# Cutting the first two token tiles at 128 columns, the last tile at 288, and changing which semaphore the last multiply waits for itself: a fused attention and MLP block on one Trainium2 core

## The chip, the cores and the metric

The kernel runs on one core of one Trainium2 chip. The metric is the device time of one execution in microseconds (us); the kernel before takes 141.5 us (median of 3 runs, 141.45 to 141.58). The span of a profile, from the first to the last instruction, is about 1.6 us shorter than that time (139.6 us in a run of 141.24). No other core works; the granted clock is 0.999 or 1.0. The engines are TensorE (PE), VectorE (DVE), ScalarE (ACT), GpSimd (POOL) and SyncE (SP). TensorE's weight loads are called PEld.

## The reference, cut to what matters

```python
xn  = layernorm(x)                                  # x: 1 x 2048 x 448, bf16
q, k, v = split(xn @ wqkv)                          # 16 heads of 28
pq, pk = phi(q), phi(k)                             # phi(t) = (t + 1 if t > 0 else exp(t)) + 1e-6
s   = (pq @ (pk.T @ v)) / (pq @ sum(pk)) @ wo       # linear attention, per head
g   = silu(relu(xn @ w1 + b1)**2 @ w2 + b2)         # hidden width 1792
out = x + s * g
```

## The kernel before

The kernel is a small program of operations with reads and writes. A list scheduler with modelled durations sets the order of the work on VectorE, ScalarE and GpSimd, and the PSUM bank of each result; TensorE's order is the order in the text. Three parts matter here.

**The head.** 16 tiles of 128 tokens. The first four tiles are normed on VectorE (the last 64 columns of tiles 0 and 1 on GpSimd), transposed on TensorE in chunks of 128 columns (0 to 3, the last only 64 wide) and copied from PSUM to SBUF as `xT`. In the first two tiles the norm of the first 384 columns is cut in two, so that TensorE can begin early. `k0`, `k1` are the key projections of tiles 0 and 1 (512 columns a matmul); `h_mains` are the first hidden units over both tiles (256 columns a matmul).

```python
def ln_norm(si, part=None):
    c = (slice(0, D if si > 3 else 384), slice(0, 256), slice(256, 384))[0 if part is None else part + 1]
    ...
reads = xn_of(t)[c // 2 :][:1] or xn_of(t) if c < 3 else [("xd", t)]      # which norm part a transpose waits for
...
warm(8, wide=True)                  # matmuls of ones, 512 columns each: the warm-up
turn("xT00", 0, (0,), "dve")        # transpose of tile 0 chunk 0, copied by VectorE
turn("xT01", 0, (1,), "act")
turn("xT02", 0, (2,), "act")
mains(k0, (0,), [("xT", 0, 0)] + wk0)
turn("xT10", 1, (0, 1), "act")
mains(k0, (1,), [("xT", 0, 1)])
turn("xT12", 1, (2,), "act")
mains(k0, (2,), [("xT", 0, 2)])
mains(k1, (0, 1), [("xT", 1, 0)] + wk0)
h_mains(0, (0, 1))
mains(k1, (2,), [("xT", 1, 2)])
...                                 # transpose of b1
h_mains(0, (2,))
turn("xT03", 0, (3,), "act", 2)
h_mains(1)
turn("xT2", 2, K3, "act")
h_mains(2)
turn("xT3", 3, K3, "dve")
h_mains(3)
turn("xT23", 2, (3,), "act", 2)
rests(k0, k1)                       # the first matmuls of 64 rows: in the trace two start 3 ns apart (8.598, 8.601 us)
```

**The waits.** The last tile's two multiplies wait in the trace for one semaphore themselves; the others are on a separate wait instruction ahead of each. The list `need` is ordered by modelled end, latest first, and the first of the list is the one that ends up on the instruction itself: the trace has ScalarE's semaphore on the last multiply, which starts at 137.336 us, and TensorE's on a separate wait at 137.270.

```python
for d in sorted(deps, key=lambda d: -d.end):
    ...
    need.append((d.sem, d.seq))
```

**The tail.** The last tile is done in two column parts, so that the second part's chain is short: bias matmul, silu on ScalarE, multiply by the attention part on VectorE, residual on VectorE, store.

```python
ca, cb = slice(0, 256), slice(256, D)
full(ss(14), KS, ["msz"])
full(gg(15, ca))
full(ss(15, ca, eng="dve", end=False), KS, ["msz"])
store(15, ca)
full(gg(15, cb, True), range(NF + 1))                     # ends with the bias matmul
full(ss(15, cb, eng="dve", end=False), KS, ["msz"])       # four matmuls of the attention part
store(15, cb, "act")
```

## Time and profile before

| what | value | from |
|---|---|---|
| time, median | 141.5 us | the runs |
| span of the profiled run | 139.6 us | page |
| TensorE busy | 98% of the span | page, part 1 |
| chain that ended last | 95% TensorE | page, part 4 |
| first transpose, first key matmul, first 64-row matmul | 4.19, 4.79, 8.60 us | timeline |
| last bias matmul, last store issued, all landed | 136.65, 138.02, 139.61 us | timeline |

The chain of the kernel before, by engine:

```profile
PE 95%; DVE 2%; DMA 2%; issue 0%; DVEq 0%
```

So time is to be had only where TensorE is not at work or works slowly. The records of single matmuls show no gap over 0.1 us between 8.6 and 137 us. What remains is the head and the tail. First the timeline of the head of the kernel before, VectorE's first norms and then TensorE, with lines left out: start in us, duration in us, engine, line, operation, out<-in, shape, count, and in brackets idle time before it.

```profile
3.82 0.59 DVE L488 TENSOR_SCALAR xn<-x_tok,mv,rstd 128x256 bf16<-128x256 bf16 x2
...
4.19 0.57 PE L531 MATMUL pb<-ident,xn 128*128 128x128 bf16 x3 [0.29 <-DVE xn L488]
4.79 0.54 PE L645 MATMUL pb<-w_qkv,xT 128*128 128x512 bf16 x1
5.17 0.28 PE L531 MATMUL pb<-ident,xn 128*128 128x128 bf16 x2
5.28 0.38 PE L645 MATMUL pb<-w_qkv,xT 128*128 128x512 bf16 x1
5.50 0.22 PE L531 MATMUL pb<-ident,xn 128*128 128x128 bf16 x1
5.55 0.97 PE L645 MATMUL pb<-w_qkv,xT 128*128 128x512 bf16 x3
6.36 0.38 PE L692 MATMUL pb<-xT,w 128*128 128x256 bf16 x2
...
8.60 0.39 PE L645 MATMUL pb<-w_qkv,xT 64*128 64x512 bf16 x2
```

The records of matmuls overlap: the one of 512 columns at 5.280 us lasts 0.379 us, and the next starts at 5.496, 0.216 us after it. So the distances between starts say more than durations. The warm-up matmuls, of 512 columns too, start 0.427 us apart (from 0.707 to 3.267 us). "Half clock" or "half rate" in this document means the distance of 0.427 us, "full clock" that of 0.216, and "the clock's rise" the moment when the one gives way to the other. The profile's own granted clock reads 1.00 in every stretch of the head (`--windows`), so that a clock lies behind the two distances is the author's reading and was not shown.

The first key matmul at 4.79 takes 0.37, to 5.17: the clock rose in the middle of it, at about 5.11 us by this arithmetic (an estimate: half rate, 0.427, up to there, full rate, 0.216, after). The three of 5.55 hide another wait: the records have the first at 5.552 and the second at 5.919, 0.151 us later than 0.216 would put it. That is the wait for ScalarE's copy xT10.

Then the tail of the kernel before, the timeline of ScalarE, VectorE and TensorE, with lines left out:

```profile
136.65 0.25 PE L958 MATMUL pb<-b2b,c 128*128 128x192 bf16 x1
...
136.94 0.33 ACT L935 ACTIVATE gbuf<-pb 128x192 bf16<-128x192 f32 x1 [0.80 <-PE pb L958]
...
137.34 0.36 DVE L995 TENSOR_TENSOR xn<-pb,gbuf 128x192 bf16<-128x192 f32 x1 [0.42 <-ACT gbuf L935]
137.73 0.26 DVE L1004 TENSOR_TENSOR xn<-xn,x_tok 128x192 bf16<-128x192 bf16 x1
138.02 0.37 ACTq L403 DMA_DIRECT2D out_dram<-xn  x1
```

The bias matmul ends, the silu follows, the multiply starts 0.070 us after the silu's end (records: 137.336 after 137.266), then residual and store. Just ahead of the multiply the records have a separate wait for TensorE's semaphore, at 137.270.

### The profile page before, as it was taken

How to read it: one execution, taken by the hardware profiler on the slowest of the kernel's cores; microseconds unless marked ns; L12 is line 12 of the kernel's file. 1: busy time of each engine (PE TensorE's matmuls, PEld its weight loads, DVE VectorE, ACT ScalarE, POOL GpSimd, SP SyncE). 2: the span in 40 equal slices, each digit the busy share in tenths (PEclk: the TensorE clock that was granted, in tenths of full speed). 3: DMA queues.
4: the chain of work that ended last, by engine and by line, in shares of the span. 5: the costliest groups of instructions: out<-in, count | busy, mean ns of one | idle time of the engine just before them, and what ended most of it. 6: DMA issues, size and time to landing. Idle time of an engine off the chain costs nothing.

```text
span 139.6 us, 3096 instructions
## 1 busy us (share of the span) xinstructions
PE 136.6 (98%) x1255; PEld 68.4 (49%) x1255; DVE 92.3 (66%) x225; ACT 78.3 (56%) x153; POOL 26.8 (19%) x35
## 2 busy tenths in 40 slices
PE   9999999999999999999999999999999999999993
PEld 2484444444444444444455455645555555555482
DVE  3989797898888996889995900217946072452743
ACT  4689789788988888979788912513033030300220
POOL 2810000000000000000893000000001429092670
DMA  6997546999722300000000149980000102112132
GB/s 207 238 335 212 94 152 171 359 285 149 130 52 58 64 9 5 0 19 5 0 0 0 34 115 161 159 137 7 0 0 5 66 0 97 40 62 69 36 100 66
DMA packets 20353, 12.90 MB, mean 92 GB/s; under 512 B 9524, under 2 KB 19956, under 8 KB 20340
## 3 DMA queue, kind: packets, MB, share of 16 engines
q1 hardware_dynamic: 18332, 11.52, 33.4%
q10 hardware_dynamic: 2008, 1.20, 4.6%
q8 instruction: 10, 0.16, 0.5%
q14 instruction: 3, 0.02, 0.1%
HBM read 8.78 MB, written 2.10 MB: 78 GB/s over the span
## 4 chain that ended last, share of the span: by engine, by line
PE 95%; DVE 2%; DMA 2%; issue 0%; DVEq 0%
PE pb L959 31%; PE pb L692 30%; PE pb L645 9%; PE pb L1025 8%; PE pb L726 7%; PE pb L676 6%; DMA x_tok<-in_A_x_dram 2%; PE pb L732 1%; PE pb L531 1%; DVE st L465 1%; PE pb L819 1%; PE pb L780 1%; PE pb L857 0%; DVE xn L995 0%; DVE mv L466 0%; PE pb L850 0%
## 5 line engine op out<-in xcount | busy, mean ns | idle before, releaser
L692 PE MATMUL pb<-xT,w 64*128 64x512 bf16 (+2 forms) x408 | 51.7, 365 | 0.0
L959 PE MATMUL pb<-w,r 64*128 64x448 bf16 (+3 forms) x406 | 44.9, 343 | 0.0
L701 ACT ACTIVATE r<-pb,b1f 128x512 bf16<-128x512 f32 x56 | 35.1, 689 | 3.7 <-PE pb L692 3.7
L692 PEld LDWEIGHTS pb<-xT,w 64*128 64x128 bf16 (+1 forms) x408 | 22.9, 94 | 22.2 <-ACT r L701 0.3
L959 PEld LDWEIGHTS pb<-w,r 64*128 64x128 bf16 (+1 forms) x406 | 22.8, 95 | 19.9 <-issue 0.7
L935 ACT ACTIVATE gbuf<-gbuf 128x448 bf16<-128x448 bf16 (+1 forms) x16 | 8.7, 566 | 36.0 <-DVE gbuf L970 35.5
L970 DVE TENSOR_TENSOR gbuf<-pb,b2b 128x448 bf16<-128x448 f32 (+1 forms) x16 | 9.2, 608 | 28.8 <-PE pb L959 28.8
L1004 POOL TENSOR_TENSOR xn<-xn,x_tok 128x448 bf16<-128x448 bf16 x15 | 15.0, 1032 | 46.3 <-DVE xn L995 46.3
L645 PE MATMUL pb<-w_qkv,xT 64*128 64x512 bf16 (+1 forms) x106 | 18.2, 378 | 0.0
L676 PE MATMUL pb<-xT,w_qkv 64*128 64x512 bf16 x84 | 15.5, 376 | 0.0
L709 DVE TENSOR_TENSOR r<-r 128x512 bf16<-128x512 bf16 x42 | 14.3, 416 | 0.0
L392 POOL MEMSET kvm<- 128x2048 bf16 x1 | 1.8, 1805 | 59.2 <-DVE zb L670 59.2
L1025 PE MATMUL pb<-msb,pqT 64*128 64x448 bf16 (+3 forms) x93 | 10.9, 343 | 0.0
L633 DVE SCALAR_TENSOR_TENSOR qk<-pb,qk 128x512 bf16<-128x512 f32 x16 | 10.6, 684 | 0.2
L465 DVE BATCH_NORM_STATS2 st<-x_tok 128x6 f32<-128x448 bf16 x16 | 9.3, 611 | 2.1 <-DMA x_tok<-in_A_x_dram 2.1
L623 ACT ACTIVATE qk<-pb 128x512 bf16<-128x512 f32 x16 | 8.9, 595 | 3.2 <-PE pb L645 2.7
L995 DVE TENSOR_TENSOR xn<-pb,gbuf 128x448 bf16<-128x448 f32 (+2 forms) x17 | 9.2, 590 | 2.0 <-ACT gbuf L935 1.5
L645 PEld LDWEIGHTS pb<-w_qkv,xT 64*128 64x128 bf16 (+1 forms) x106 | 6.7, 94 | 6.3 <-ACT xT L545 0.3
L726 PE MATMUL pb<-qk,xn 128*128 128x448 bf16 x48 | 9.3, 353 | 0.0
L676 PEld LDWEIGHTS pb<-xT,w_qkv 64*128 64x128 bf16 x84 | 6.0, 94 | 5.0
L710 ACT ACTIVATE r<-r 128x512 bf16<-128x512 bf16 x14 | 8.4, 636 | 0.0
L623 ACT ACTIVATE pqT<-pb 128x512 bf16<-128x512 f32 x12 | 6.8, 597 | 2.7 <-PE pb L692 1.6
(72 smaller groups left out, 101.9 us busy)
## 6 DMA issues: line engine op xcount, KB each, us to landing
out_dram<-xn SPq DMA_DIRECT2D x15, 112.0 KB, 1.7
w<-in_B_w_dram SPq DMA_DIRECT2D x1, 1568.0 KB, 9.9
x_tok<-in_A_x_dram SPq DMA_DIRECT2D x3, 448.0 KB, 3.7
xT<-rows ACTq DMA_DIRECT2D x6, 112.0 KB
w<-in_B_w_dram SPq DMA_DIRECT2D x1, 576.0 KB, 5.6
xT<-rows SPq DMA_DIRECT2D x5, 112.0 KB
w_o<-in_A_wo_dram SPq DMA_DIRECT2D x1, 392.0 KB, 11.0
w_qkv<-in_A_wqkv_dram SPq DMA_DIRECT2D x1, 384.0 KB, 3.4
```

The lines of the kernel that those rows point to most:

```text
L465: add("dve", lambda e, _: e.bn_stats(st6[:, si, :], x_tok[:, si, :]), [("x", si)], [("st", si)], 0.58),
L623: add("act", lambda e, _: e.activation(out=slot, in_=src(), func=AF.Exp), [buf, "actw"], [tile], 0.6)
L633: lambda e, _: e.scalar_tensor_tensor(out=slot, in0=src(), scalar=1.0 + 1e-6, in1=slot, op0=ALU.add, op1=ALU.max),
L645: return e.matmul(ps(b)[:, 0:512], xT[half[h], c, si * P : (si + 1) * P], w_qkv[half[h], c, 384 : 2 * D], start=start, stop=stop,)
L676: return e.matmul(ps(b)[:, 0:512], w_qkv[half[h], c, m * P : (m + 1) * P], xT[half[h], c, g * 512 : (g + 1) * 512], start=start, stop=stop,)
L692: return e.matmul(ps(b)[:, c0 : c0 + n], w_1[half[h], c, fi * P : (fi + 1) * P], xT[half[h], c, t : t + n], start=start, stop=stop,)
L701: lambda e, _: e.activation(out=slot, in_=ps(b)[:, 0:512], func=AF.Relu, bias=b1f[:, fi : fi + 1]),
L709: return e.tensor_tensor(out=slot, in0=slot, in1=slot, op=ALU.mult)
L726: last = e.matmul(ps(b)[:, 0:D], xn[:, si, c * P : (c + 1) * P], pk_of(si), start=(si == 0), stop=(si == NT - 1),)
L959: return e.matmul(ps(b)[:, 0:n], r2[half[h], fi, si * P : (si + 1) * P], w_2[half[h], fi, c], start=start, stop=stop)
L1004: eng, lambda e, _: e.tensor_tensor(out=ob, in0=ob, in1=x_tok[:, si, c], op=ALU.add),
L1025: return e.matmul(ps(b)[:, 0:n], q, m, start=start, stop=stop)
```

## The change

Its intent: TensorE should start earlier and in smaller steps in the head (the first norm has 128 columns instead of 256, and one transpose instead of two is due before tile 1's first copy). At the end the last part should be smaller (160 columns instead of 192), and the multiply should have TensorE's semaphore on itself, with ScalarE's on the separate wait.

```diff
-            for d in sorted(deps, key=lambda d: -d.end):
+            for d in sorted(deps, key=lambda d: (d.eng != op.lastly, -d.end)):
...
-            c = (slice(0, D if si > 3 else 384), slice(0, 256), slice(256, 384))[...]
+            c = (slice(0, D if si > 3 else 384), slice(0, P), slice(P, 384))[...]
...
-                reads = xn_of(t)[c // 2 :][:1] or xn_of(t) if c < 3 else [("xd", t)]
+                reads = xn_of(t)[min(c, 1) :][:1] or xn_of(t) if c < 3 else [("xd", t)]
...                                              # finish(): the multiply
+            if c.stop == D and c.start:
+                op.lastly = "pe"
...
-        turn("xT10", 1, (0, 1), "act")
+        turn("xT10", 1, (0,), "act")
         mains(k0, (1,), [("xT", 0, 1)])
-        turn("xT12", 1, (2,), "act")
+        turn("xT12", 1, (1, 2), "act")
         mains(k0, (2,), [("xT", 0, 2)])
-        mains(k1, (0, 1), [("xT", 1, 0)] + wk0)
-        h_mains(0, (0, 1))
-        mains(k1, (2,), [("xT", 1, 2)])
+        mains(k1, (0,), [("xT", 1, 0)] + wk0)
+        h_mains(0, (0,))
+        mains(k1, (1, 2), [("xT", 1, 1)])
...
-        h_mains(0, (2,))
+        h_mains(0, (1, 2))
...
-        ca, cb = slice(0, 256), slice(256, D)
+        ca, cb = slice(0, 288), slice(288, D)
```

More of the change, by code (lines that the diff above doesn't have):

```diff
@@ L45, in __init__ @@
         self.first = False
+        self.lastly = None
 class Acc:
@@ L484, in ln_norm @@
         def ln_norm(si, part=None):
-            c = (slice(0, D if si > 3 else 384), slice(0, 256), slice(256, 384))[0 if part is None else part + 1]
+            c = (slice(0, D if si > 3 else 384), slice(0, P), slice(P, 384))[0 if part is None else part + 1]
             return add(
@@ L492, in ln_norm @@
                 [("x", si), ("mv", si), ("rstd", si)], [("xn", si) if part is None else ("xn", si, part)],
-                0.4 if part is None else (0.22, 0.18)[part],
+                0.4 if part is None else (0.14, 0.24)[part],
             )
@@ L992, in finish @@
             n = c.stop - c.start
-            add(
+            op = add(
                 "dve",
```

## The prediction

> **What bounds the kernel.** The chain of waits is 95% TensorE. In the trace's matmul records I find no gap over 0.1 us between 8.6 and 137 us. So only the head (3.8 to 8.6 us) and the tail (after 136.6 us) can give time. The timeline of the head shows TensorE waiting 0.14 us (4.27 to 4.46), 0.27 us (4.52 to 4.79, for VectorE's copy xT00) and 0.15 us (5.77 to 5.92, for ScalarE's copy xT10); the first key matmul also takes 0.37 us instead of 0.216, because the clock is at half rate until about 5.1 us[...] (warm-up matmuls of 512 columns start 427 ns apart, later ones 216 ns). [...]
>
> **Head.** The norm of 256 columns takes 314 ns, of 384 columns 349: 0.27 ns a column, so 128 instead of 256 saves about 35 ns (estimate). The first transpose (4.19), the copy xT00 (4.51) and the first key matmul (4.79) come 35 ns earlier, of which the half-rate clock leaves about half. The transposes of chunks 1 and 2 both wait for the second norm part (done at 4.41 as now), so xT01's copy starts 0.17 us later, still before its use at 5.2. Tile 1: one transpose (56 ns) leaves the space before the second key matmul, and the copy xT10 falls from 384 to 272 ns, done at about 5.68; the 0.15 us wait at 5.77 goes. In exchange xT12's copy is 384 ns instead of 272, done at about 6.12: TensorE, with one chunk of the first hidden matmuls instead of two to fill with, waits a new 0.10 us before tile 1's second key matmul. Net: the transpose xT03 (6.96) moves to about 6.88. The weight loads have landed in time, xn3 (7.76, 50 ns before its use) moves up 35 ns, so 0.08 us should hold to 8.6 us and shift the dense part as a whole.
>
> **Tail.** TensorE's columns are the same in total; its last matmul ends about 13 ns earlier[...]. After the bias matmul come 4 matmuls of 160 columns (69 ns each) instead of 192 (82 ns); the silu falls from 331 to about 304 ns but starts 40 ns later, ending 14 ns later. Now TensorE's semaphore is waited for ahead of the last multiply (at 137.270), which starts 66 ns after, and ScalarE's (silu over at 137.266) on the instruction; a direct wait costs 33 ns after ScalarE. In the changed kernel TensorE arrives about 60 ns before ScalarE, and ScalarE's wait moves to the separate instruction: the multiply starts about 100 ns after silu's end, 45 ns later than now. Multiply (358 to 324) and residual (258 to 241) give 50 ns back. Tail: about -0.01 us. The swap alone looks like a loss of about 60 ns, hidden by the smaller part. The 288-column chain on VectorE ends near 137.23, just clear.
>
> **Sum.** -0.08 - 0.01: 141.4 us from 141.5, range 141.15 to 141.6. Faster by over 2%: 0.005; within 2%: 0.99; slower: 0.005.
>
> **Signs.** Timeline: first transpose near 4.15; no wait at 5.75 but one near 6.1; first 64-row matmul at 8.52 instead of 8.60; last multiply 320 ns, starting 0.10 us after silu's end.
>
> **What would make it wrong.** The scheduler orders VectorE's and ScalarE's work and the PSUM banks by modelled times; another order could give TensorE a wait in the dense part. The clock's rise could fall elsewhere. The 288-column chain might block the last multiply. The separate wait may cost less than 66 ns.

## The result, and the profile after

The changed kernel takes 141.29 us (median of 6 runs, 141.15 to 141.68), the kernel before 141.50 (6 runs, 141.38 to 141.58). The ratio is 0.999 with a 95% interval of 0.9976 to 1.0004. Ratios here are the mean time of one kernel's fast runs over that of the other's of the same rounds, so not quite the ratio of the medians. Executions over 1.5% slower than the fastest of the same kernel are left out of the means.

The profiled runs (141.24 us before, below all six of its timed runs, and 141.17 after) differ by 0.087 us from the first instruction to the landing of the last store. The order of the instructions on each engine differs only in the moved and resized pieces, so the scheduler did not reorder the dense part. The chain is still TensorE's:

```profile
PE 95%; DVE 2%; DMA 2%; ACT 0%; issue 0%; DVEq 0%
```

The timeline of the head of the changed kernel, the corresponding lines:

```profile
3.81 0.59 DVE L489 TENSOR_SCALAR xn<-x_tok,mv,rstd 128x128 bf16<-128x128 bf16 x2
...
4.15 0.70 PE L532 MATMUL pb<-ident,xn 128*128 128x128 bf16 x3 [0.25 <-DVE xn L489]
4.76 0.47 PE L646 MATMUL pb<-w_qkv,xT 128*128 128x512 bf16 x1
5.07 0.22 PE L532 MATMUL pb<-ident,xn 128*128 128x128 bf16 x1
5.12 0.38 PE L646 MATMUL pb<-w_qkv,xT 128*128 128x512 bf16 x1
5.34 0.28 PE L532 MATMUL pb<-ident,xn 128*128 128x128 bf16 x2
5.46 0.59 PE L646 MATMUL pb<-w_qkv,xT 128*128 128x512 bf16 x2
5.89 0.27 PE L693 MATMUL pb<-xT,w 128*128 128x256 bf16 x1
6.09 0.60 PE L646 MATMUL pb<-w_qkv,xT 128*128 128x512 bf16 x2
...
8.50 0.39 PE L646 MATMUL pb<-w_qkv,xT 64*128 64x512 bf16 x2
```

The first transpose comes 35 ns earlier. There is no wait inside the 5.46 group any more. A new one stands between 5.89 and 6.09: a matmul of 256 columns takes 0.109 us from start to start (6.593 to 6.702), so 0.097 us are idle (the copy xT12). The first key matmul takes 0.31 us to 5.07, not 0.37: the clock rose earlier in this run, at about 4.95 (estimated in the same way). The first 64-row matmul starts at 8.499 us instead of 8.598.

The tail of the changed kernel, the same lines of the timeline:

```profile
136.62 0.23 PE L959 MATMUL pb<-b2b,c 128*128 128x160 bf16 x1
...
136.89 0.30 ACT L936 ACTIVATE gbuf<-pb 128x160 bf16<-128x160 f32 x1 [0.59 <-PE pb L959]
...
137.30 0.33 DVE L996 TENSOR_TENSOR xn<-pb,gbuf 128x160 bf16<-128x160 f32 x1 [0.17 <-ACT gbuf L936]
137.66 0.24 DVE L1007 TENSOR_TENSOR xn<-xn,x_tok 128x160 bf16<-128x160 bf16 x1
137.94 0.37 ACTq L404 DMA_DIRECT2D out_dram<-xn  x1
```

The multiply now starts 0.103 us after the silu's end (137.301 after 137.198), not 0.070.

The 0.087 us, section by section, from the records of the two profiles:

| section | before, us | after, us | difference |
|---|---|---|---|
| to the first norm | 3.817 | 3.811 | -0.006 |
| first norm to first 64-row matmul | 4.781 | 4.688 | -0.093 |
| from there to the last bias matmul | 128.055 | 128.126 | +0.071 |
| bias matmul to issue of the last store | 1.365 | 1.310 | -0.055 |
| issue to landing seen | 1.591 | 1.587 | -0.004 |

In the third row, 0.053 us is only a shift: 18 matmuls of the first part (14 of the MLP, 4 of the attention) have 32 columns more and 14 of the second part have 32 fewer, and 128 columns take 0.053 us (a matmul of 512 columns takes 0.216 us from start to start, one of 256 takes 0.109, so 128 columns more are half of 0.107). e2 and e12, which have the split, show 128.109 in this row. The other 0.018 arises at about 16.7 us, where one of two matmuls that run side by side starts 0.017 us later than in e2. So the tail as a whole, third row's shift included, gained about 0.002 us, and the head gained 0.093 in this pair of profiles. The experiments ask whether the head's part belongs to the change, and why a smaller last part gained nothing.

### The profile page after: what moved, and what is told of

Its sections match the earlier page's. It is cut to its first block, busy times and chain, and to the rows that moved or that the text cites. A ratio compares the mean times of both kernels' runs of the same rounds, so it can differ in the third digit from the quotient of the medians.

```text
span 139.5 us, 3096 instructions
## 1 busy us (share of the span) xinstructions
PE 136.6 (98%) x1255; PEld 72.4 (52%) x1255; DVE 92.3 (66%) x225; ACT 78.3 (56%) x153; POOL 26.8 (19%) x35
## 3 DMA queue, kind: packets, MB, share of 16 engines
q10 hardware_dynamic: 2008, 1.19, 4.6%
## 4 chain that ended last, share of the span: by engine, by line
PE 95%; DVE 2%; DMA 2%; ACT 0%; issue 0%; DVEq 0%
PE pb L960 31%; PE pb L693 30%; PE pb L646 9%; PE pb L1028 8%; PE pb L727 7%; PE pb L677 6%; DMA x_tok<-in_A_x_dram 2%; PE pb L733 1%; PE pb L532 1%; DVE st L466 1%; PE pb L820 1%; PE pb L781 1%; PE pb L858 0%; DVE mv L467 0%; DVE xn L996 0%; PE pb L851 0%
## 5 line engine op out<-in xcount | busy, mean ns | idle before, releaser
L693 PEld LDWEIGHTS pb<-xT,w 64*128 64x128 bf16 (+1 forms) x408 | 25.2, 94 | 19.3 <-issue 0.3
## 6 DMA issues: line engine op xcount, KB each, us to landing
w_o<-in_A_wo_dram SPq DMA_DIRECT2D x1, 392.0 KB, 11.4
```

Source lines behind the costliest of these rows:

```text
L693: return e.matmul(ps(b)[:, c0 : c0 + n], w_1[half[h], c, fi * P : (fi + 1) * P], xT[half[h], c, t : t + n], start=start, stop=stop,)
```

## The experiments

Twelve kernels ran, each correct. Theory: the head is worth something, the tail nothing because the swap of the waits costs what the smaller part gives. Rivals: the gain is the tail's; or the swap helps; or the head's gain is the luck of a clock that rose earlier.

The timed ratios alone could not decide. In the first group the runs of the kernel before spread from 141.1 to 142.59 us, so every interval is about 0.3% to either side. The decisions below rest on the records of the profiles, which repeat to a few ns in the tail (1.365 us before and in e1, 1.251 and 1.249 in e2 and e4, from the bias matmul to the store's issue). The timed results are in the table at the end of the section.

### e1: the head alone

The edit is the changed kernel with the tail undone:

```diff
-        ca, cb = slice(0, 288), slice(288, D)
+        ca, cb = slice(0, 256), slice(256, D)
-            if c.stop == D and c.start:
-                op.lastly = "pe"
```

> Only the head part of the change (norm, transposes and copies of the first two tiles). Theory (the gain is the head's): first 64-row matmul near 8.50 to 8.54 us instead of 8.60, the wait at 5.77 gone, one of 0.10 us near 6.0 instead; the tail as before, last multiply 70 ns after the silu's end; total 0.06 to 0.10 us less than before. Rival (the gain is the tail's): total as before. Second rival (the clock's rise, 5.12 us before and 4.95 after, was the luck of one profile): the start of the 64-row part follows the rise, and with a rise at 5.1 it is at 8.60 as before.

The tail was as before: bias matmul to store issue 1.365 us, multiply 0.071 us after the silu. The head missed the expected place: first 64-row matmul at 8.913, 5.170 us after the first norm, not 4.69. The records show matmuls of 512 columns 0.427 us apart as late as 5.20; the clock rose only at about 6.22 us. So the second rival had a point: where the clock rises decides more of the head than the change does.

TensorE also waited 0.23 us further on. The list of waits of e1 between 8 and 13 us, and then its timeline of TensorE there:

```profile
DVE st L466 <- DMA x_tok<-in_A_x_dram: 0.5, 1, 0.5
PEld pb L693 <- DVE qk L634: 0.5, 1, 0.5
```

```profile
10.89 1.03 PE L646 MATMUL pb<-w_qkv,xT 64*128 64x512 bf16 x8
11.98 1.04 PE L693 MATMUL pb<-xT,w 64*128 64x512 bf16 x8
```

VectorE waited for tiles 4 to 7 of x, which landed at 9.45 us in this run (8.61 before, 8.67 after). Its statistics of tiles 4 and 5 stand in its order ahead of the work on the first keys (8.64 and 9.18 us, then 9.79, in the profile before), and ScalarE's variance of those tiles stands in ScalarE's order ahead of its first relu (10.17, then 10.45). The first hidden matmul of 512 columns waits for both, by the records: the relu ended at 11.881 us and VectorE's work at 11.753, the matmul started at 11.981. So ScalarE's came last, though the list names VectorE, whose semaphore is on the instruction itself. Experiment e10 tests that the landing holds this chain.

### e2, e3, e4: the split, the swap, and the change without the swap

e2 is the kernel before with one line changed, e3 the kernel before with the swap alone, e4 the changed kernel without it:

```diff
 e2   -        ca, cb = slice(0, 256), slice(256, D)
 e2   +        ca, cb = slice(0, 288), slice(288, D)
 e3   -            for d in sorted(deps, key=lambda d: -d.end):
 e3   +            for d in sorted(deps, key=lambda d: (d.eng != op.lastly, -d.end)):
 e3   +            if c.stop == D and c.start:
 e3   +                op.lastly = "pe"
 e4   (from the changed kernel)
 e4   -            if c.stop == D and c.start:
 e4   -                op.lastly = "pe"
```

> Only the last tile's parts 288 and 160, no swap of the semaphores. Theory: the last multiply waits for ScalarE on itself and starts about 35 to 45 ns after the silu's end (TensorE's separate wait came about 60 ns earlier), takes 325 ns instead of 358, the residual 243 instead of 258; counted from the end of the matmuls the tail is about 0.06 us shorter than before. Rival (the split alone gives nothing without the swap): under 0.02 us shorter.

> Only the swap, with parts 256 and 192. Theory (the separate wait costs some 66 ns and here moves to ScalarE, which comes last): last multiply about 100 ns after the silu's end instead of 70, total 0.03 us longer than before. Rival (the swap helps, as intended): multiply starts earlier than 70 ns after the silu's end, total shorter.

> The changed kernel without the swap. Theory: last multiply 35 to 45 ns after the silu's end instead of 102, everything after it about 0.06 us earlier: total 0.06 us less than the changed kernel, 0.14 less than before. Rival: the swap is worth something, and this is slower than the changed kernel.

The silu and the multiply in the timelines, first e2 (split only):

```profile
137.22 0.30 ACT L935 ACTIVATE gbuf<-pb 128x160 bf16<-128x160 f32 x1 [0.59 <-PE pb L958]
137.57 0.33 DVE L995 TENSOR_TENSOR xn<-pb,gbuf 128x160 bf16<-128x160 f32 x1
```

e3 (swap only):

```profile
136.92 0.33 ACT L936 ACTIVATE gbuf<-pb 128x192 bf16<-128x192 f32 x1 [0.80 <-PE pb L959]
137.35 0.36 DVE L996 TENSOR_TENSOR xn<-pb,gbuf 128x192 bf16<-128x192 f32 x1 [0.45 <-ACT gbuf L936]
```

e4 (the change without the swap):

```profile
137.38 0.30 ACT L936 ACTIVATE gbuf<-pb 128x160 bf16<-128x160 f32 x1 [0.59 <-PE pb L959]
137.73 0.32 DVE L996 TENSOR_TENSOR xn<-pb,gbuf 128x160 bf16<-128x160 f32 x1
```

From the records:

| kernel | parts | separate wait for | multiply after silu's end | bias matmul to store issue | with the 0.053 us shift |
|---|---|---|---|---|---|
| before | 256, 192 | TensorE | 0.070 us | 1.365 us | 1.365 |
| e1 | 256, 192 | TensorE | 0.071 | 1.365 | 1.365 |
| e3 | 256, 192 | ScalarE | 0.103 | 1.397 | 1.397 |
| after | 288, 160 | ScalarE | 0.103 | 1.310 | 1.363 |
| e2 | 288, 160 | TensorE | 0.044 | 1.251 | 1.304 |
| e4 | 288, 160 | TensorE | 0.043 | 1.249 | 1.302 |

The theory holds to a few ns. The swap alone costs 0.032 us at the old parts and 0.061 at the new ones (1.310 less 1.249); the split alone gives 0.061. The two cancel. The reason is read from the order of arrival: ScalarE's semaphore comes last in all six, and a semaphore on a separate wait costs about 66 ns from that wait's start to the start of the instruction (137.270 to 137.336 before, 137.235 to 137.301 after), against 33 ns from the silu's end to the multiply of the first part before (136.137 to 136.170), where ScalarE's semaphore is on the instruction and comes long after the others (the separate wait for them was over at 135.710). In this tail the separate wait should therefore stand for the engine that arrives first. At 192 columns TensorE was only 37 ns ahead (last matmul over at 137.229, silu at 137.266), so before the change its separate wait still showed; at 160 columns it is 63 ns ahead (137.135 and 137.198 after), and its wait is nearly hidden in e2 and e4. The swap puts ScalarE, the last, there instead.

Two things in these runs were not expected. e2's clock rose late (about 5.9 us, first 64-row matmul at 8.841). e4 had two extra waits in the dense part: 0.065 us at 11.4 (x landed at 8.88) and 0.41 us at 97.3, for which e4's list of waits between 94 and 98.5 us shows again VectorE behind a transfer:

```profile
DVE pqT L921 <- DMA xT<-rows: 3.8, 1, 3.8
PEld pb L960 <- DVE gbuf L971: 0.7, 1, 0.7
```

In the kernel before the same wait for the transfer was 3.4 us and TensorE lost nothing visible there. This wait varies with the transfer; e4's longer total in its profile (span 140.0) is not the price of leaving the swap out.

### e5, e6: both heads at the full clock; e11, e12: both at half clock

To take the moment of the clock's rise out, e5 and e6 are the kernel before and the changed one with 20 more warm-up matmuls ahead, and the first statistics waiting for them:

```diff
+        warm(20, wide=True, gate=["gate"])
         warm(8, wide=True)
...
-  ... bn_stats(st6[:, si, :], x_tok[:, si, :]), [("x", si)], [("st", si)], 0.58)
+  ... bn_stats(st6[:, si, :], x_tok[:, si, :]), [("x", si)] + (["gate"] if si == 0 else []), [("st", si)], 0.58)
```

> The kernel before with 20 more warm-up matmuls, and the first statistics made to wait for them, so that the whole head runs at the full clock with its data long landed. Theory: counted from the start of the first norm, the waits for xT00 and xT10's copies are there as before, and the first 64-row matmul starts near 4.6 us.

> The changed kernel, the same way. Theory (half of the head's gain seen in the first pair of profiles came from a clock that rose 0.16 us earlier there): counted from the start of the first norm, the first 64-row matmul comes 0.03 us earlier than in the kernel before, not 0.10, because the second key matmul now waits 0.06 us for xT01's late copy and tile 1's second key matmul 0.10 us for xT12's. Rival (the parts themselves are worth 0.10 us): 0.10 us earlier.

The first norms and the first 64-row matmul in the timeline of e5:

```profile
9.06 0.59 DVE L488 TENSOR_SCALAR xn<-x_tok,mv,rstd 128x256 bf16<-128x256 bf16 x2
...
13.74 0.39 PE L645 MATMUL pb<-w_qkv,xT 64*128 64x512 bf16 x2
```

and of e6:

```profile
8.26 0.59 DVE L489 TENSOR_SCALAR xn<-x_tok,mv,rstd 128x128 bf16<-128x128 bf16 x2
...
12.91 0.39 PE L646 MATMUL pb<-w_qkv,xT 64*128 64x512 bf16 x2
```

By the records 13.737 - 9.064 = 4.673 us and 12.910 - 8.264 = 4.646: the changed head is 0.027 us shorter, not 0.093. TensorE is at the full clock in both (a matmul of 512 columns takes 0.22 us, 10.38 to 10.60, in e5; two take 0.43, 9.85 to 10.28, in e6). After the first key matmul starts, TensorE's waits add up to 0.235 us in e5 (0.055, then 0.151 for xT10's copy, then 0.029 for xn3) and to 0.242 in e6 (0.023, 0.065 for xT01's copy, 0.097 for xT12's, 0.057 for xn3). The change moved the waits; it did not take them away. The totals of these two runs, 147.06 and 145.91, say nothing: the warm-up itself ran partly at half clock (to about 6 us in e5, 4.3 in e6), and each had a different wait for a transposing transfer near 43 us.

e11 and e12 are the opposite: the two kernels with the warm-up taken out.

```diff
-        warm(8, wide=True)
```

> The kernel before without the warm-up matmuls, so that the head runs at half clock. Theory: no wait for xT10's copy; the transposes of chunk 3 of tiles 0 and 1 start about 4.6 us after the first norm.

> The changed kernel the same way. Theory: at half clock TensorE is the limit in the head, no wait for copies after the first key matmul in either kernel, so the transposes of chunk 3 come only the 0.03 us of the shorter first norm earlier. Rival: the parts are worth 0.1 us at any clock.

The first norms and the chunk-3 transposes in the timelines of e11:

```profile
3.76 0.59 DVE L488 TENSOR_SCALAR xn<-x_tok,mv,rstd 128x256 bf16<-128x256 bf16 x2
...
8.34 0.42 PE L531 MATMUL pb<-ident,xn 128*128 128x128 bf16 x2
```

and e12:

```profile
3.84 0.59 DVE L489 TENSOR_SCALAR xn<-x_tok,mv,rstd 128x128 bf16<-128x128 bf16 x2
...
8.38 0.42 PE L532 MATMUL pb<-ident,xn 128*128 128x128 bf16 x2
```

By the records 8.340 - 3.764 = 4.576 us and 8.384 - 3.836 = 4.548: 0.028 us. Neither has a wait for a copy after the first key matmul, as expected: at half clock (the second key matmul takes 0.43 us to the next start, 5.35 to 5.78 in e11 and 5.29 to 5.72 in e12) TensorE itself is the limit here. The clock rose at about 8.7 us in e12 and 9.0 in e11, after the point compared; the times to the first 64-row matmul (6.513 and 6.347 us) therefore do not compare.

There is a third comparison at early rises, found and not made. e3 has the old head, and its clock rose between about 4.5 and 4.9 us: its copy xT00 still came 0.324 us after the first transpose, as in the kernel before (0.326; 0.268 in e5). Its first key matmul gives no closer moment, because the transposes after it waited for VectorE's norm (they start 0.057 us after its end, 0.058 in e5). The changed kernel's clock rose at about 4.95, and that of e10, which has the same head, before 4.8. From the first norm to the first 64-row matmul e3 takes 4.713 us, the other two 4.688 and 4.686: 0.025 to 0.027 (e3 and e10 ran on different chips, 15 and 4; what that does was not measured, so this pair is weaker than the two made ones).

| kernel | head | clock's rise, us (estimate from the starts) | first norm to first 64-row matmul, us |
|---|---|---|---|
| e5 | old | before the head | 4.673 |
| e3 | old | 4.5 to 4.9 | 4.713 |
| before | old | 5.11 | 4.781 |
| e2 | old | 5.9 | 4.977 |
| e6 | new | before the head | 4.646 |
| e4 | new | before 4.6 | 4.643 |
| e10 | new | 4.5 to 4.8 | 4.686 |
| after | new | 4.95 | 4.688 |
| e1 | new | 6.22 | 5.170 |

Within one head, the moment of the rise is worth up to 0.5 us (4.643 us in e4, 5.170 in e1). So a part of the 0.093 us between the first two profiles belongs to a clock that rose 0.17 us earlier, and how large a part depends on where one counts. At the later profile's clock the change is worth about 0.025 and the clock the other 0.07. What the change is worth at a rise of 5.11 us, the clock of the kernel before, was not measured. An estimate from the records: the new head's first key matmul (4.76) would end 0.08 us later than it did, and the wait for xn3 of 0.04 us and the 0.01 us that the restart after it costs (0.066 us from the matmul at 7.786 to the next, against 0.056) would be gone; the head would take about 4.72 us, 0.06 less than before, and 0.03 would be the clock's. The clocks that were held equal give 0.025 to 0.028.

Why so little even at the full clock: xT3's transposes wait for VectorE's norm of tile 3. From the first norm to the first of these transposes it takes 3.959 us in e5, 4.001 in e3, 3.934 in e6 and 3.975 after. TensorE stands at that point in all four, so it is VectorE's chain of statistics and norms that ends last there, and the change shortens it only by 25 ns (the first norm itself is 32 ns shorter). In the profile before, with its later clock, TensorE came to these transposes at 4.078 us and did not wait; the norm would have allowed about 4.00 (an estimate: its end at 7.761, and the 0.057 us after it in e3).

### e10: the landing of tiles 4 to 7, made later

```diff
+        spare = sb("spare", [P, 4, D], bf)
+        add("sp", lambda e, _: e.dma_start(spare[:, :, :], x_r[:, 8:12, :]), [], ["spare"], 0.01, nbytes=1)
         load_x(4, 8)
```

> The changed kernel with one more load of 448 KB (into a buffer that nothing reads) ahead of the load of tiles 4 to 7; the orders of VectorE and TensorE are the same. Theory: those tiles land about 1.5 us later, near 10.3, and the first 512-column hidden matmul starts 2.5 us after the landing, near 12.8 instead of 11.34: TensorE waits about 1.4 us there. Rival (that matmul hangs on something else, or has slack): it stays within 0.3 us of 11.4.

The waits of e10 between 9 and 14 us, and then the timeline of TensorE:

```profile
DVE st L468 <- DMA x_tok<-in_A_x_dram: 1.5, 1, 1.5
PEld pb L695 <- DVE qk L636: 1.5, 1, 1.5
```

```profile
10.47 1.03 PE L648 MATMUL pb<-w_qkv,xT 64*128 64x512 bf16 x8
12.53 0.82 PE L695 MATMUL pb<-xT,w 64*128 64x512 bf16 x6 [1.03 <-ACT rstd L482]
```

The tiles landed at 10.00 us (1.3 us later than in the changed kernel, a little less than expected) and the matmul started at 12.53. That is 2.53 us after the landing, as in e1 (11.98 after 9.45) and e4 (11.41 after 8.88). TensorE lost 1.19 us. The profile names VectorE's work on the keys in one view and ScalarE's rstd in the other. By the records VectorE's work ended 0.228 us before the matmul and ScalarE's first relu 0.100 us before it, the same in e1, e4 and e10: the relu comes last, and it stands behind ScalarE's variance, which waits for VectorE's statistics and so for the landing. VectorE's first keys' work kept its place behind the statistics: it began at 11.18 us although ScalarE's part of it was done at 9.52. e9, below, moves the statistics back and has no wait at this matmul. So in this order an earlier TensorE is worth something only while x lands early: the matmul wants to start 2.84 us after the first 64-row matmul (11.34 and 8.50 after), and what lies before landing + 2.53 is given back.

### e7, e8, e9: trying for more

e7 is e4 with the transpose of b1 put into the new wait, and the last three hidden matmuls put before xT3's transposes, which wait for VectorE. e8 also cuts the load of tiles 4 to 7 in two. e9 is e7 with the statistics of tiles 4 and 5 behind the first keys' work.

```diff
 e7   -        mains(k1, (1, 2), [("xT", 1, 1)])
 e7            ...                                       # transpose of b1
 e7   +        mains(k1, (1, 2), [("xT", 1, 1)])
 e7   -        turn("xT3", 3, K3, "dve")
 e7            h_mains(3)
 e7   +        turn("xT3", 3, K3, "dve")
 e8   -        load_x(4, 8)
 e8   +        load_x(4, 6)
 e8   +        load_x(6, 8)
 e9   -                            op.after = [head["xT3"]]
 e9   +                            op.after = [head["xT3"]] + [o for o in early if o.eng == "dve"]
```

> The changed kernel without the swap, the transpose of b1 moved into the wait before tile 1's second key matmul, and the last three hidden matmuls put before xT3's transposes, which wait for the norm of tile 3. Theory: the first 64-row matmul 0.08 to 0.10 us earlier than in the changed kernel at the same clock; but the first 512-column hidden matmul cannot start before 2.53 us after tiles 4 to 7 of x have landed (11.98 after 9.45 and 11.41 after 8.88 in two runs), so where they land after about 8.7 us the gain is lost there.

> As e7_fill, with the load of tiles 4 to 7 cut into two loads. Theory: tiles 4 and 5 land about 0.5 us earlier, VectorE's statistics no longer hold the release of the bank, no wait near 11.4 us; total 0.15 to 0.25 us less than before.

> As e7_fill, with the statistics of tiles 4 and 5 put behind VectorE's work on the first two key tiles, so that the release of their bank no longer stands behind the landing of x. Theory: no wait of TensorE near 11.4 us however late x lands, tail as in e7_fill; total 0.15 us less than before where the clocks rise alike. Risk: the later norms of tiles 4 to 7 make a wait later.

The reordering did what it should in the head: e8 and e9, whose clocks rose before 4.75 us, take 4.523 and 4.524 us from the first norm to the first 64-row matmul, 0.12 less than e4 and e6. (e7's profile had a late clock, 5.9 us, and does not compare.) Both then gave it back. In e8 the additional load pushed the weights of the next hidden units back: the last of them landed at 11.14 us (10.33 in e7, 10.50 after), the matmul that waits for them through two separate waits started at 11.35, 0.14 us late, and the time is 141.46, not faster than before. (The profile's list names ScalarE for this wait, because its semaphore is the one on the instruction itself; the records show the separate wait for the weights ending at 11.18.) In e9 the transposing transfers of tiles 4 to 7 were issued at 15.48 us instead of 13.51 in e7; e9's waits between 21 and 24 us:

```profile
PEld pb L646 <- DMA xT<-xn: 1.2, 1, 1.2
```

TensorE lost 0.87 us there and the kernel is 0.6% slower. e7 has the lowest median of all, 141.03 against 141.33 in its group, but its interval holds 1. It is not shown to be faster; what is shown is its tail, 1.249 us, 0.061 shorter than the changed kernel's.

| kernel | median, us | before, same group | ratio of means, 95% interval |
|---|---|---|---|
| changed | 141.29 | 141.50 | 0.999 (0.9976 to 1.0004) |
| e1 head alone | 141.41 | 141.62 | 0.9988 (0.9959 to 1.0016) |
| e2 split alone | 141.29 | 141.62 | 0.9977 (0.9947 to 1.0006) |
| e3 swap alone | 141.47 | 141.62 | 1.0 (0.9966 to 1.0034) |
| e4 without swap | 141.47 | 141.62 | 0.9986 (0.9959 to 1.0014) |
| e7 | 141.03 | 141.33 | 0.9991 (0.9972 to 1.001) |
| e8 | 141.46 | 141.33 | 1.0013 (0.9996 to 1.003) |
| e9 | 142.14 | 141.33 | 1.0063 (1.0046 to 1.008) |

e5, e6, e10, e11 and e12 were not timed in rounds and were read for their profiles alone.

## Why the prediction was right or wrong

**The time and the class were right.** 141.4 was predicted, in a range of 141.15 to 141.6; 141.29 was measured, "same". That the two profiles differ by 0.087 us, so close to the forecast of 0.09, was partly the luck of the clock, as the head shows.

**What bounds the kernel: right.** In the first two profiles the dense part from the first 64-row matmul to the last bias matmul kept its length to 0.02 us, apart from the 0.053 us that the split moves across its end.

**The tail: right, step by step.** The prediction had the silu at 304 ns, the multiply about 100 ns after it and 324 ns long, the residual at 241, the whole tail at -0.01 us, and the swap alone as a loss of about 60 ns. Measured: 304, 103, 325, 243, about -0.002 (or -0.006 with the landing), and 61. e3 and e4 show the loss directly.

**The head: the waits were named rightly, the size was not the change's.** The new wait of 0.10 us was predicted near 6.1 and came at 6.00 to 6.09 (0.098); the one at 5.77 went; the first transpose came at 4.15; the first 64-row matmul at 8.50 against a predicted 8.52. But the step that gave "0.08 us" was mis-sized: with the clock held equal, high or low, the head is 0.027 and 0.028 us shorter, and 0.025 to 0.027 at early rises; at the prediction's own 5.1 us it would be about 0.06 by the estimate above, which no run tested. Two parts of that step failed. First, it treated the rise at 5.1 us as a fixed point of the kernel. Nothing shows that the change moves it, but it differs between runs with the same head, from 4.5 to 4.9 us in e3 to 5.9 in e2. Over all runs with the same warm-up, whose first matmul starts at 0.30 us, it lies between about 3.2 us (e9: the last two of its 8 warm-up matmuls start 404 ns apart instead of 427, and the last takes 381 ns instead of 634) and about 6.2 us (e1), and the two first profiles happened to differ by 0.17 us in the right direction. Second, it said that xn3 was 50 ns ahead of its use and would stay clear. In the profile after, TensorE waits 0.04 us for it at 7.79; at the full clock this wait, with those for xT01 and xT12, takes back what the absent wait for xT10 gave.

**What it left out.** The prediction checked the weight loads but not the load of tiles 4 to 7 of x: other work stands behind it in the order of VectorE and ScalarE, and TensorE's matmul started 2.53 us after the landing in e1, e4 and e10. In e1 and e4 its landing cost TensorE 0.23 and 0.065 us, against the 0.03 to 0.06 us that is to be won.

**Stays open.** Whether the measured difference of the means (0.14 us) is more than the 0.03 us that the profiles account for at an equal clock (about 0.06 by the estimate at 5.1 us): the interval, 0.9976 to 1.0004, holds both, and zero. Why TensorE waited 0.41 us near 97 us in e4's profile beyond the late transfer that VectorE waited for was not followed further.

## What to carry to other kernels

Where an instruction must wait for two engines, let the one that arrives last be on the instruction itself and put the earlier one on the separate wait (in this tail the other way round cost 32 and 61 ns); then count the hop of the separate wait (66 ns here) as part of the earlier path. A smaller step in a pipeline's start is worth only what it takes off the chain that ends last; add up all waits after it, before and after, to see whether they went or moved. And before explaining a gain of 0.1 us by an edit, find what else differs between the two profiles: here the clock's rise was worth 0.03 to 0.07 of it, depending on where one counts, and holding the clock equal in both kernels brought it to light.
